# Moving loads, crossbar transposes and state updates between slots of a hand-ordered schedule

## The chip, the core and the metric

The kernel runs on one core of a Trainium2 chip. The metric is the device time of one execution in microseconds. Five executions of the kernel before are at hand, with a median of 217.74 us. Times inside the profile count from the first instruction of one profiled execution.

## What is computed

Causal attention with a decay, in blocks, followed by a two-layer MLP with ELU. The reference, cut to what matters:

```python
batch, n_heads, seq, head_dim = (4, 8, 768, 64)
for b in range(nb):                       # blocks of the sequence
    intra = einsum('bhic,bhjc->bhij', qb, kb) * Dmask
    intra = einsum('bhij,bhjd->bhid', intra, vb)
    inter = einsum('bhid,bhde->bhie', qb * lam_pow, kv_state)
    out[:, :, sl] = intra + inter
    kv_state = lam_block * kv_state + einsum('bhsd,bhse->bhde', kb * rev_pow, vb)
x = out.transpose(0, 2, 1, 3).reshape(3072, 512)
h = x @ w_in                              # 512 x 2048
g = where(h > 0, h, exp(min(h, 0)) - 1)
return g @ w_out                          # 2048 x 512
```

Everything goes in and comes out in float32; the matmuls work in float16.

## The kernel before

The sequence is cut into six chunks of 128 positions. A group g is one chunk of one batch element (g = 4 * chunk + batch), so there are 24 groups. Each turns into 128 rows of the MLP's input. Groups are handled two at a time ("group 10" below is the pair 10 and 11), and the MLP works on seven tiles of TS = 4, 2, 4, 4, 4, 4, 2 groups.

For a pair of groups the attention does the following, one function for each:

- `emit_load` (line 61): three DMAs from GpSimd's queue (POOL) bring q, k and v from HBM, cast to float16 (qn, kn, vn).
- q and k are transposed to qT and kT. For groups up to 6 TensorE does it (`att_T`, `att_Te`), from group 8 on two transposing DMAs from SyncE's queue (SP), the crossbar transposes (`att_xT`, line 272, issued at line 277).
- `att_kd` (line 283) scales k by the decay (kd), on VectorE (DVE) or, for group 8, ScalarE (ACT).
- `att_S` (line 303): scores psS of one group on TensorE (PE, line 308); `att_mask` (line 314) multiplies by the decay mask on DVE, giving P (line 320).
- `att_O` (line 326): output psO of both groups from P and v (line 334) and from qT and the state st (line 342). `att_X` copies it, scaled, to xt, the MLP's input, on DVE (line 363). These are the copies that the change's name speaks of.
- `att_U` (line 369): the state's increment psU from kd and v (line 380). `att_st` (line 404) updates the state st on DVE, in eight instructions (line 418). The next chunk of the same batch elements, four groups on, reads it.

The MLP: `mm1` gives one 128-column slice n of psH for a tile t (line 441; line 459 for the tiles of two groups). ACT takes exp (line 470, e) and relu (line 474, r) of it, and DVE joins them to g (`elu`, line 487). `mm2` (line 519) adds slice n of g times wo to psM for one group of the tile; after the 16th slice psM is copied to osb (DVE at line 533, ACT at line 535; six buffers) and stored from SP's queue (line 536).

The order of the instructions on every engine is the order of the program; nothing reorders them. It is written out by hand in the list `steps`: each entry is a slot, such as (2, 5), with the `mm1` of that slot, then what `at(slot, ...)` has put there, run by `do(s)`, then `elu`, then the slot's list of `mm2`. Within a slot, what was put there first runs first. `visit(g, s0, s1, s2)` puts a pair's parts into three slots: kd in s0, scores and masks in s1, output, increment, copy and update in s2. The table `XT` says in which slot a pair's crossbar transposes are emitted; that fixes their place in SP's queue relative to the stores.

Loads of groups 10 and up are paced: `paced_load` (line 659) has POOL first copy one element of a g made one step earlier (line 665), so that the three DMAs after it start no earlier than that g.

Scores, outputs and increments share the PSUM tag "S", two buffers of two banks; psM and psH have two banks each. With `bufs=3`, qT and kT have three buffers each, which the pairs use in turn.

Of the kernel before, what the change touches and what calls it, by code (L numbers as in the profile page):

```python
# [7 lines left out]
FP32 = mybir.dt.float32  # L8
FP16 = mybir.dt.float16
I32 = mybir.dt.int32  # L10
AF = mybir.ActivationFunctionType
ALU = mybir.AluOpType
# [3 lines left out]
def kernel(  # L16
# [10 lines left out]
    nc = tc.nc  # L27

    B, H, S, D = q.shape
    L = 128  # L30
    HP = H // 2
# [5 lines left out]
    TS = [4, 2, 4, 4, 4, 4, 2]  # L37
# [8 lines left out]
    asb = ctx.enter_context(tc.tile_pool(name="asb", bufs=2))  # L46
    msb = ctx.enter_context(tc.tile_pool(name="msb", bufs=1))
# [67 lines left out]
    def run_loads(items):  # L115
# [25 lines left out]
        out=ident16[:], in0=rel[:], scalar1=0.0, scalar2=None, op0=ALU.is_equal  # L141
    )
    nc.vector.tensor_scalar(
        out=causT[:], in0=rel[:], scalar1=0.0, scalar2=None, op0=ALU.is_ge
# [81 lines left out]
    def att_Te(g, n, which, eng):  # L226
        j = "qk".index(which)
        pt = pT.pop((g, j))
        dst = asb.tile([128, n, HP, 128], FP16, tag=f"{which}T", name=f"{which}T{g}", bufs=3)
        if eng == "v":  # L230
            nc.vector.tensor_copy(dst[:], pt)
        else:
            nc.scalar.copy(out=dst[:], in_=pt)
        for i in range(n):
            (qT, kT)[j][g + i] = dst[:, i]

    def att_T2(g, which, tag):

        j = "qk".index(which)
        nat = heads((qn, kn)[j], g)  # L240
        dst = asb.tile([128, 1, HP, 128], FP16, tag=f"{which}T", name=f"{which}T{g}", bufs=3)
        w = HP // 2
        for x in range(2):
            t1 = ps.tile([128, w, 128], FP16, tag=tag, bufs=2, name=f"psT{which}{g}_{x}")
            for y in range(w):
                hp = x * w + y
                nc.tensor.transpose(
                    t1[:, y, :], in_=nat[:, 2 * hp : 2 * hp + 2, :], identity=ident16[:]
                )
            copy = nc.vector.tensor_copy if x else nc.scalar.copy  # L250
            copy(out=dst[:, 0, x * w : (x + 1) * w], in_=t1[:])
        (qT, kT)[j][g] = dst[:, 0]
# [19 lines left out]
    def att_xT(g):  # L272

        for j, ts in enumerate((qn, kn)):
            w = "qk"[j]
            dst = asb.tile([128, 2 * HP, 128], FP16, tag=f"{w}T", name=f"{w}T{g}", bufs=3)
            nc.sync.dma_start_transpose(
                out=dst[:], in_=heads(ts, g, 2).rearrange("p h d -> p (h d)")
            )
            for i in range(2):  # L280
                (qT, kT)[j][g + i] = dst[:, i * HP : (i + 1) * HP]
# [150 lines left out]
    def mm1_mm(t, n, lo, hi, tag="H"):  # L432

        if n == 0 and lo == 0:
            gt[t] = msb.tile([128, NF, TS[t] * L], FP16, tag="g", bufs=2, name=f"g{t}")
        if lo == 0:
            pH_of[t, n] = ps.tile([128, TS[t] * L], FP32, tag=tag, bufs=2, name=f"psH{t}_{n}")
        pH = pH_of[t, n]
        wi, j = wi_t[wi_at[n][0]], wi_at[n][1]
        for kk in range(HP):  # L440
            nc.tensor.matmul(  # L441
                pH[:, lo:hi], lhsT=wi[:, kk, j * 128 : (j + 1) * 128],
                rhs=xt[t][:, kk, lo:hi], start=(kk == 0), stop=(kk == HP - 1),
            )

    def mm1(t, n, alt=False):

        MT = TS[t] * L
        if MT == 256:
            if n == 0:  # L450
                gt[t] = msb.tile([128, NF, MT], FP16, tag="g", bufs=2, name=f"g{t}")
            pH = ps.tile(
                [128, 2 * MT], FP32, tag="M" if (t, n) in ((1, 0),) else "H", bufs=2,
                name=f"psH{t}_{n}",
            )
            for x in range(2):
                wi, j = wi_t[wi_at[n + x][0]], wi_at[n + x][1]
                for kk in range(HP):
                    nc.tensor.matmul(  # L459
                        pH[:, x * MT : (x + 1) * MT],  # L460
                        lhsT=wi[:, kk, j * 128 : (j + 1) * 128],
                        rhs=xt[t][:, kk, :], start=(kk == 0), stop=(kk == HP - 1),
                    )
            MT *= 2
        else:
            if (t, n) not in pH_of:
                mm1_mm(t, n, 0, MT, "M" if t == 0 and n % 2 == 0 and n < 8 else "H")
            pH = pH_of.pop((t, n))
        e = msb.tile([128, MT], FP32, tag="e", bufs=3, name=f"e{t}_{n}")
        nc.scalar.activation(e[:], pH[:], AF.Exp)  # L470
        if alt:
            return e, None, pH
        r = msb.tile([128, MT], FP16, tag="r", bufs=3, name=f"r{t}_{n}")
        nc.scalar.activation(r[:], pH[:], AF.Relu)  # L474
        return e, r, pH

    def elu(t, n, e, r, pH):
# [11 lines left out]
        )  # L489

    def mm2_last(t, i):

        c, b = divmod(T0[t] + i, B)
        t0 = b * S + c * L
        x0 = 0
        for x, (w, tag) in enumerate([(384, 'M'), (128, 'H')]):
            pm = ps.tile([128, w], FP32, tag=tag, bufs=2, name=f"psM{t}_{i}_{x}")
            for n in range(NF):
                nc.tensor.matmul(  # L499
                    pm[:], lhsT=gt[t][:, n, i * L : (i + 1) * L],  # L500
                    rhs=wo_t[wo_at[n][0]][:, wo_at[n][1], x0 : x0 + w],
                    start=(n == 0), stop=(n == NF - 1),
                )
            o = msb.tile([128, w], FP32, tag="osb", bufs=6, name=f"osl{x}")
            (nc.scalar.copy if x % 2 else nc.vector.tensor_copy)(o[:], pm[:])
            (nc.scalar if x % 2 else nc.sync).dma_start(
                out=out[t0 : t0 + L, x0 : x0 + w], in_=o[:]
            )
            x0 += w
# [47 lines left out]
    def at(s, f, *a, **k):  # L557
        run.setdefault(s, []).append(lambda: f(*a, **k))

    def do(s):  # L560
        for f in run.pop(s, []):
            f()
# [41 lines left out]
    op_Te(3, "k")  # L604
    cut = {}
    for x, f in zip([('O', 0), ('S', 3), ('qs', 0), ('O', 1), ('qs', 1), ('O', 2), ('qs', 2), ('qs', 3), ('O2', 3, 'S'), ('L', 0, 384)], W[8:]):
        warm(f, "M" if not cut else "S")
        if x[0] == "O":
            att_O(x[1], 1, "M" if x[1] < 2 or not cut else "S")
            att_X(x[1], 1)  # L610
        elif x[0] == "S":
            att_S(x[1])
            att_mask(x[1], 2)
        elif x[0] == "qs":
            late_qs(x[1], x[1] + 1)
        elif x[0] == "O2":
            att_OX2(x[1], x[2])
        elif x[0] == "L":
            lo = cut.get(x[1], 0)
            mm1_mm(0, x[1], lo, x[2], "M" if x[1] % 2 == 0 else "H")  # L620
            cut[x[1]] = x[2]

    run_loads(LOADS[16:28])
# [7 lines left out]

    XT = {8: ('B', 12), 10: (1, 12), 12: (2, 4), 14: (2, 12), 16: (3, 4), 18: (3, 12), 20: (4, 4), 22: (4, 12)}
    TMPS = {}

    def visit(g, s0, s1, s2):
        if g in XT:
            at(XT[g], att_xT, g)
        else:
            at(s0, att_T, g, 2, "q")
            at(s0, att_T, g, 2, "k")  # L640
            at(s0, att_Te, g, 2, "q", "a")
            at(s0, att_Te, g, 2, "k", "v" if g in () else "a")
        if g not in ():
            at(s0, att_kd, g, 2, "p" if g in () else "a" if g in (8,) else "v")
        at(s1, att_S, g)
        at(s1, att_S, g + 1)
        at(s1, att_mask, g)
        at(s1, att_mask, g + 1)
        if g in ():
            at(s1, att_kd, g, 2, "p" if g in () else "a" if g in (8,) else "v")  # L650
        at(s2, att_O, g, 2)
        at(s2, att_U, g)
        at(s2, att_X, g, 2)
        at(s2, att_st, g)
        at(TMPS.get(g, s2), att_tmp, g + B)

# [10 lines left out]

    for s, a, b in [(('B', 2), 28, 29), ((1, 2), 29, 30), ((1, 10), 30, 31), ((2, 3), 31, 32), ((2, 11), 32, 33), ((3, 3), 33, 34), ((3, 11), 34, 35), ((4, 3), 35, 36)]:
        at(s, paced_load, s, LOADS[a:b])

    steps = [(('A', 0), (0, 0), []), (('A', 1), (0, 1), []), (('A', 2), (0, 2), []), (('A', 3), (0, 3), []), (('A', 4), (0, 4), []), (('A', 5), (0, 5), []), (('A', 6), (0, 6), []), (('A', 7), (0, 7), []), (('A', 8), (0, 8), []), (('A', 9), (0, 9), []), (('A', 10), (0, 10), [(0, 0, 0), (0, 1, 0)]), (('A', 11), (0, 11), [(0, 0, 1), (0, 1, 1)]), (('A', 12), (0, 12), [(0, 0, 2), (0, 1, 2)]), (('A', 13), (0, 13), [(0, 0, 3), (0, 1, 3)]), (('A', 14), (0, 14), [(0, 0, 4), (0, 1, 4)]), (('A', 15), (0, 15), [(0, 0, 5), (0, 1, 5)]), (('B', 0), None, [(0, 2, 0), (0, 2, 1), (0, 2, 2), (0, 2, 3)]), (('B', 1), None, [(0, 2, 4), (0, 2, 5), (0, 3, 0), (0, 3, 1)]), (('B', 2), None, [(0, 3, 2), (0, 3, 3), (0, 3, 4), (0, 3, 5)]), (('B', 3), None, [(0, 0, 6), (0, 1, 6), (0, 2, 6), (0, 3, 6)]), (('B', 4), None, [(0, 0, 7), (0, 1, 7), (0, 2, 7), (0, 3, 7)]), (('B', 5), None, [(0, 0, 8), (0, 1, 8), (0, 2, 8), (0, 3, 8)]), (('B', 6), None, [(0, 0, 9), (0, 1, 9), (0, 2, 9), (0, 3, 9)]), (('B', 7), None, [(0, 0, 10), (0, 1, 10), (0, 2, 10), (0, 3, 10)]), (('B', 8), None, [(0, 0, 11), (0, 1, 11), (0, 2, 11), (0, 3, 11)]), (('B', 9), None, [(0, 0, 12), (0, 1, 12), (0, 0, 13), (0, 1, 13)]), (('B', 10), None, [(0, 0, 14), (0, 1, 14), (0, 0, 15), (0, 1, 15)]), (('B', 11), None, [(0, 2, 12), (0, 3, 12), (0, 2, 13), (0, 3, 13)]), (('B', 12), None, [(0, 2, 14), (0, 3, 14), (0, 2, 15), (0, 3, 15)]), ((1, 0), (1, 0), []), ((1, 2), (1, 2), []), ((1, 4), (1, 4), []), ((1, 6), (1, 6), [(1, 0, 0), (1, 1, 0), (1, 0, 1), (1, 1, 1)]), ((1, 8), (1, 8), [(1, 0, 2), (1, 1, 2), (1, 0, 3), (1, 1, 3)]), ((1, 10), (1, 10), [(1, 0, 4), (1, 1, 4), (1, 0, 5), (1, 1, 5)]), ((1, 12), (1, 12), [(1, 0, 6), (1, 1, 6), (1, 0, 7), (1, 1, 7)]), ((1, 14), (1, 14), [(1, 0, 8), (1, 1, 8), (1, 0, 9), (1, 1, 9)]), ((2, 0), (2, 0), [(1, 0, 10), (1, 0, 11)]), ((2, 1), (2, 1), [(1, 0, 12), (1, 0, 13)]), ((2, 2), (2, 2), [(1, 0, 14), (1, 0, 15), (1, 1, 10)]), ((2, 3), (2, 3), [(1, 1, 11), (1, 1, 12)]), ((2, 4), (2, 4), [(1, 1, 13), (1, 1, 14)]), ((2, 5), (2, 5), [(1, 1, 15), (2, 0, 0), (2, 0, 1)]), ((2, 6), (2, 6), [(2, 0, 2), (2, 0, 3)]), ((2, 7), (2, 7), [(2, 0, 4)]), ((2, 8), (2, 8), [(2, 0, 5), (2, 1, 0)]), ((2, 9), (2, 9), [(2, 0, 6), (2, 1, 1)]), ((2, 10), (2, 10), [(2, 0, 7), (2, 1, 2)]), ((2, 11), (2, 11), [(2, 0, 8), (2, 1, 3)]), ((2, 12), (2, 12), [(2, 0, 9), (2, 1, 4)]), ((2, 13), (2, 13), [(2, 0, 10), (2, 1, 5)]), ((2, 14), (2, 14), [(2, 0, 11), (2, 1, 6)]), ((2, 15), (2, 15), [(2, 0, 12), (2, 1, 7)]), ((3, 0), (3, 0), [(2, 0, 13), (2, 1, 8), (2, 0, 14), (2, 1, 9)]), ((3, 1), (3, 1), [(2, 0, 15), (2, 1, 10), (2, 1, 11), (2, 1, 12)]), ((3, 2), (3, 2), [(2, 1, 13), (2, 1, 14), (2, 1, 15), (2, 2, 0)]), ((3, 3), (3, 3), [(2, 2, 1), (2, 2, 2), (2, 2, 3), (2, 2, 4), (2, 2, 5)]), ((3, 4), (3, 4), [(2, 2, 6), (2, 2, 7), (2, 2, 8), (2, 2, 9)]), ((3, 5), (3, 5), [(2, 2, 10), (2, 2, 11), (2, 2, 12), (2, 2, 13)]), ((3, 6), (3, 6), [(2, 2, 14), (2, 2, 15), (2, 3, 0), (2, 3, 1), (2, 3, 2)]), ((3, 7), (3, 7), [(2, 3, 3), (2, 3, 4), (2, 3, 5), (2, 3, 6)]), ((3, 8), (3, 8), [(2, 3, 7), (2, 3, 8), (2, 3, 9), (2, 3, 10)]), ((3, 9), (3, 9), [(2, 3, 11), (2, 3, 12), (2, 3, 13), (2, 3, 14), (2, 3, 15)]), ((3, 10), (3, 10), [(3, 0, 0), (3, 0, 1), (3, 0, 2), (3, 0, 3)]), ((3, 11), (3, 11), [(3, 0, 4), (3, 0, 5), (3, 1, 0), (3, 0, 6)]), ((3, 12), (3, 12), [(3, 1, 1), (3, 0, 7), (3, 1, 2), (3, 0, 8), (3, 1, 3)]), ((3, 13), (3, 13), [(3, 0, 9), (3, 1, 4), (3, 0, 10), (3, 1, 5)]), ((3, 14), (3, 14), [(3, 0, 11), (3, 1, 6)]), ((3, 15), (3, 15), [(3, 0, 12), (3, 1, 7)]), ((4, 0), (4, 0), [(3, 0, 13), (3, 1, 8), (3, 0, 14), (3, 1, 9)]), ((4, 1), (4, 1), [(3, 0, 15), (3, 1, 10), (3, 1, 11), (3, 1, 12)]), ((4, 2), (4, 2), [(3, 1, 13), (3, 1, 14), (3, 1, 15), (3, 2, 0)]), ((4, 3), (4, 3), [(3, 2, 1), (3, 2, 2), (3, 2, 3), (3, 2, 4), (3, 2, 5)]), ((4, 4), (4, 4), [(3, 2, 6), (3, 2, 7), (3, 2, 8), (3, 2, 9)]), ((4, 5), (4, 5), [(3, 2, 10), (3, 2, 11), (3, 2, 12), (3, 2, 13)]), ((4, 6), (4, 6), [(3, 2, 14), (3, 2, 15), (3, 3, 0), (3, 3, 1), (3, 3, 2)]), ((4, 7), (4, 7), [(3, 3, 3), (3, 3, 4), (3, 3, 5), (3, 3, 6)]), ((4, 8), (4, 8), [(3, 3, 7), (3, 3, 8), (3, 3, 9), (3, 3, 10)]), ((4, 9), (4, 9), [(3, 3, 11), (3, 3, 12), (3, 3, 13), (3, 3, 14), (3, 3, 15)]), ((4, 10), (4, 10), [(4, 0, 0), (4, 0, 1), (4, 0, 2), (4, 0, 3)]), ((4, 11), (4, 11), [(4, 0, 4), (4, 0, 5), (4, 1, 0), (4, 0, 6)]), ((4, 12), (4, 12), [(4, 1, 1), (4, 0, 7), (4, 1, 2), (4, 0, 8), (4, 1, 3)]), ((4, 13), (4, 13), [(4, 0, 9), (4, 1, 4), (4, 0, 10), (4, 1, 5)]), ((4, 14), (4, 14), [(4, 0, 11), (4, 1, 6)]), ((4, 15), (4, 15), [(4, 0, 12), (4, 1, 7)]), ((5, 0), (5, 0), [(4, 0, 13), (4, 1, 8), (4, 0, 14), (4, 1, 9)]), ((5, 1), (5, 1), [(4, 0, 15), (4, 1, 10), (4, 1, 11), (4, 1, 12)]), ((5, 2), (5, 2), [(4, 1, 13), (4, 1, 14), (4, 1, 15), (4, 2, 0)]), ((5, 3), (5, 3), [(4, 2, 1), (4, 2, 2), (4, 2, 3), (4, 2, 4), (4, 2, 5)]), ((5, 4), (5, 4), [(4, 2, 6), (4, 2, 7), (4, 2, 8), (4, 2, 9)]), ((5, 5), (5, 5), [(4, 2, 10), (4, 2, 11), (4, 2, 12), (4, 2, 13)]), ((5, 6), (5, 6), [(4, 2, 14), (4, 2, 15), (4, 3, 0), (4, 3, 1), (4, 3, 2)]), ((5, 7), (5, 7), [(4, 3, 3), (4, 3, 4), (4, 3, 5), (4, 3, 6)]), ((5, 8), (5, 8), [(4, 3, 7), (4, 3, 8), (4, 3, 9), (4, 3, 10)]), ((5, 9), (5, 9), [(4, 3, 11), (4, 3, 12), (4, 3, 13), (4, 3, 14), (4, 3, 15)]), ((5, 10), (5, 10), [(5, 0, 0), (5, 0, 1), (5, 0, 2), (5, 0, 3)]), ((5, 11), (5, 11), [(5, 0, 4), (5, 0, 5), (5, 1, 0), (5, 0, 6)]), ((5, 12), (5, 12), [(5, 1, 1), (5, 0, 7), (5, 1, 2), (5, 0, 8), (5, 1, 3)]), ((5, 13), (5, 13), [(5, 0, 9), (5, 1, 4), (5, 0, 10), (5, 1, 5)]), ((5, 14), (5, 14), [(5, 0, 11), (5, 1, 6)]), ((5, 15), (5, 15), [(5, 0, 12), (5, 1, 7)]), ((6, 0), (6, 0), [(5, 0, 13), (5, 1, 8), (5, 0, 14), (5, 1, 9), (5, 0, 15)]), ((6, 2), (6, 2), [(5, 1, 10), (5, 1, 11), (5, 1, 12), (5, 1, 13), (5, 1, 14)]), ((6, 4), (6, 4), [(5, 1, 15), (5, 2, 0), (5, 2, 1), (5, 2, 2), (5, 2, 3), (5, 2, 4)]), ((6, 6), (6, 6), [(5, 2, 5), (5, 2, 6), (5, 2, 7), (5, 2, 8), (5, 2, 9)]), ((6, 8), (6, 8), [(5, 2, 10), (5, 2, 11), (5, 2, 12), (5, 2, 13), (5, 2, 14)]), ((6, 10), (6, 10), [(5, 2, 15), (5, 3, 0), (5, 3, 1), (5, 3, 2), (5, 3, 3), (5, 3, 4)]), ((6, 12), (6, 12), [(5, 3, 5), (5, 3, 6), (5, 3, 7), (5, 3, 8), (5, 3, 9)]), ((6, 14), (6, 14), [(5, 3, 10), (5, 3, 11), (5, 3, 12), (5, 3, 13), (5, 3, 14), (5, 3, 15)]), (('E', 0), None, [(6, 0, 0), (6, 0, 1), (6, 0, 2), (6, 0, 3), (6, 0, 4), (6, 0, 5), (6, 0, 6), (6, 0, 7), (6, 0, 8), (6, 0, 9), (6, 0, 10), (6, 0, 11), (6, 0, 12), (6, 0, 13), (6, 0, 14), (6, 0, 15), (6, 1, 0), (6, 1, 1), (6, 1, 2), (6, 1, 3), (6, 1, 4), (6, 1, 5), (6, 1, 6), (6, 1, 7), (6, 1, 8), (6, 1, 9), (6, 1, 10), (6, 1, 11), (6, 1, 12), (6, 1, 13), (6, 1, 14), (6, 1, 15)])]
    for s, m1, m2 in steps:
        er = None
        if m1 is not None:
            t, n = m1
            if t == 0 and n in cut:
                mm1_mm(0, n, cut[n], TS[0] * L)
            er = mm1(t, n, alt=t == 0 and n in (2, 4, 6))
        do(s)
        if er:  # L680
            elu(t, n, *er)
        for t2, i2, n2 in m2:
            mm2(t2, i2, n2, "H" if t2 == 0 and m1 is None and i2 > 1 else "M")
# [31 lines left out]
```

## Time and profile before

| what | us |
|---|---|
| median of five runs | 217.74 |
| the five runs | 213.72, 217.94, 218.27, 213.56, 217.74 |
| the profiled execution | 213.72 |
| its span, first to last instruction | 212.0 |
| busy: PE, DVE, ACT, POOL | 203.0, 148.0, 128.3, 61.9 |
| DMA issue to landing, q of a pair, median | 7.2 |
| DMA issue to landing, transposes of q and of k, median | 4.8, 4.8 |

In the profile's rows, "L441" is line 441 of the kernel. A row of the timeline gives start and length in us, engine, line, operation, what it writes and reads, its form, the number of instructions merged into it, and in brackets how long the engine had been idle before it and what ended that. Matmuls overlap each other in such rows: a 128x512 one is shown with 0.38 us, while the next starts 0.216 us after it. A queue's rows (SPq) are the issuing of DMAs; their landing is given apart. The chain of waits is the work that ended last, followed back to its start.

### The profile page before, as it was taken

Reading aid. Unit: us, or ns where it says so; the run is one execution under the profiler, and the core shown is the slowest. Engines: PE = TensorE matmul, PEld = TensorE weight load, DVE = VectorE, ACT = ScalarE, POOL = GpSimd, SP = SyncE. Lnnn points to the kernel's source line nnn. Section 1 sums busy time; section 2 is a strip of 40 time slices with the busy share of each in tenths; the row PEclk is TensorE's granted clock in tenths of the full one; section 3 lists DMA queues with packets and bytes.
Section 4 is the critical chain, followed back from the end, with each engine's and each line's share of the span. In section 5 each row is a group of like instructions: output and inputs, shape, how many; then the busy total and the mean of one; then the engine's idle time right before and its main releaser. Section 6 shows DMA issues by size and latency. Waiting matters only on the chain.

```text
span 212.0 us, 4157 instructions
## 1 busy us (share of the span) xinstructions
PE 203.0 (96%) x1654; PEld 107.4 (51%) x1654; DVE 148.0 (70%) x240; ACT 128.3 (61%) x247; POOL 61.9 (29%) x70
## 2 busy tenths in 40 slices
PE   4887999999999999999999999999999999999994
PEld 2653444556865453534544544544544544466643
DVE  6674896566989999998698598677557634344321
ACT  6787788406784767666464666464567476675520
POOL 8999965400445070330600700600000000011000
PEclk9999999999999999999999999999999999999999
DMA  5999999999999999895699991799401111011112
GB/s 36 144 152 180 182 199 164 200 157 184 246 134 166 153 129 176 93 122 80 107 154 145 128 116 53 112 152 145 89 0 52 50 49 49 5 49 49 49 53 101
DMA packets 100756, 24.40 MB, mean 115 GB/s; under 512 B 93056, under 2 KB 97920, under 8 KB 100736
## 3 DMA queue, kind: packets, MB, share of 16 engines
q0 software_dynamic: 80384, 14.16, 85.3%
q1 hardware_dynamic: 20208, 9.90, 21.5%
q8 instruction: 13, 0.21, 0.4%
q10 hardware_dynamic: 144, 0.07, 0.1%
q14 instruction: 7, 0.06, 0.1%
HBM read 27.27 MB, written 6.29 MB: 158 GB/s over the span
## 4 chain that ended last, share of the span: by engine, by line
PE 81%; POOL 6%; DVE 5%; DMA 3%; ACT 2%; issue 1%; POOLq 0%; ACTq 0%
PE psM L519 36%; PE psH L441 30%; PE psH L459 5%; DMA wi<-in_moe_w_in_dram 3%; PE psO L334 2%; PE psS L308 2%; PE psO L342 2%; POOL qn L72 2%; POOL kn L72 2%; PE psM L499 2%; POOL vn L72 2%; DVE g L487 1%; DVE xt L363 1%; DVE P L320 1%; ACT kd L293 1%; PE psU L380 1%
## 5 line engine op out<-in xcount | busy, mean ns | idle before, releaser
L519 PE MATMUL psM<-wo,g 128*128 128x512 f16 x368 | 94.2, 380 | 0.3 <-DVE osb L533 0.3
L470 ACT ACTIVATE e<-psH 128x512 f32<-128x512 f32 x96 | 57.3, 597 | 60.2 <-PE psH L441 51.2
L487 DVE SCALAR_TENSOR_TENSOR g<-e,r 128x512 f16<-128x512 f32 x93 | 63.4, 698 | 37.2 <-ACT r L474 36.9
L441 PE MATMUL psH<-xt,wi 128*128 128x512 f16 (+2 forms) x324 | 81.4, 377 | 1.7 <-DMA wi<-in_moe_w_in_dram 1.3
L474 ACT ACTIVATE r<-psH 128x512 f16<-128x512 f32 x93 | 55.1, 593 | 0.0
L519 PEld LDWEIGHTS <-g 128*128 128x128 f16 x368 | 34.2, 98 | 38.7 <-DVE g L487 1.9
L441 PEld LDWEIGHTS <-wi 128*128 128x128 f16 x324 | 31.1, 98 | 40.1 <-DMA wi<-in_moe_w_in_dram 1.8
L320 DVE TENSOR_TENSOR P<-psS,mask 128x1024 f16<-128x1024 f32 (+1 forms) x28 | 28.7, 1066 | 5.8 <-PE psS L308 5.7
L665 POOL COPY pace<-g 1x1 f16<-1x1 f16 x7 | 2.8, 397 | 68.7 <-DVE g L487 68.7
L418 DVE SCALAR_TENSOR_TENSOR st<-st,up_p,psU 64x128 f16<-64x128 f16 x64 | 18.2, 344 | 0.1
L536 POOL DMA_DIRECT2D out_dram<-osb x2 | 1.1, 570 | 56.0 <-ACT osb L535 51.9
L363 DVE TENSOR_TENSOR xt<-psO,qs 128x1024 f16<-128x1024 f32 x10 | 12.2, 1224 | 7.2 <-PE psO L342 7.2
L459 PE MATMUL psH<-xt,wi 128*128 128x256 f16 x128 | 16.4, 273 | 0.0
L72 POOL DMA_DIRECT2D qn<-in_q_dram x14 | 15.3, 1094 | 3.7 <-DMA wi<-in_moe_w_in_dram 1.7
L72 POOL DMA_DIRECT2D vn<-in_v_dram x14 | 15.3, 1108 | 1.8 <-DMA wo<-in_moe_w_out_dram 1.8
L72 POOL DMA_DIRECT2D kn<-in_k_dram x14 | 15.3, 1091 | 1.3 <-DMA kn<-in_k_dram 1.1
L459 PEld LDWEIGHTS <-wi 128*128 128x128 f16 x128 | 12.4, 98 | 4.2
L535 ACT COPY osb<-psM 128x512 f32<-128x512 f32 x12 | 7.1, 591 | 12.2 <-PE psM L519 12.2
L334 PEld LDWEIGHTS <-vn 128*64 128x64 f16 x184 | 9.5, 109 | 4.5 <-issue 4.2
L334 PE MATMUL psO<-P,vn 128*64 128x128 f16 x184 | 11.5, 222 | 0.1
L342 PE MATMUL psO<-qT,st 128*64 128x128 f16 x160 | 10.0, 219 | 0.0
L547 PE MATMUL psW<-ident 128*128 128x256 f16 x34 | 8.0, 360 | 1.7 <-DVE ident L140 1.7
(58 smaller groups left out, 118.8 us busy)
## 6 DMA issues: line engine op xcount, KB each, us to landing
out_dram<-osb SPq DMA_DIRECT2D x21, 256.0 KB, 2.3
qn<-in_q_dram POOLq DMA_DIRECT2D x10, 256.0 KB, 7.2
kn<-in_k_dram POOLq DMA_DIRECT2D x10, 256.0 KB, 9.0
vn<-in_v_dram POOLq DMA_DIRECT2D x10, 256.0 KB, 9.1
wo<-in_moe_w_out_dram POOLq DMA_DIRECT2D x3, 512.0 KB, 14.4
wi<-in_moe_w_in_dram POOLq DMA_DIRECT2D x2, 512.0 KB, 8.3
wi<-in_moe_w_in_dram POOLq DMA_DIRECT2D x3, 256.0 KB, 6.8
qn<-in_q_dram POOLq DMA_DIRECT2D x4, 128.0 KB, 4.8
```

The costliest lines, as they stand in the source:

```text
L72: nc.gpsimd.dma_start(out=dst, in_=src[b : b + n, :, rows].rearrange("b h p d -> p (b h) d"))
L320: nc.vector.tensor_tensor(out=P[:, :, c], in0=s[:, :, c], in1=(mask if g < B else mask1)[:, :, c], op=ALU.mult,)
L334: nc.tensor.matmul(po[r, i, hp, :], lhsT=v_of(g + i, 2 * hp + hh), rhs=P[:, hh, hp, :], start=True, stop=(c == 0), skip_group_check=True,)
L342: nc.tensor.matmul(po[r, i, hp, :], lhsT=st[(g + i) % B // 2][c % 2][:, (g + i) % 2, hp, r], rhs=qT[g + i][:, hp, :], start=False, stop=Tr ...
L363: nc.vector.tensor_tensor(out=dst, in0=po[:, :, c], in1=qs[:, c].unsqueeze(1).broadcast_to([128, n, w, 128]), op=ALU.mult,)
L418: nc.vector.scalar_tensor_tensor(out=new[r, :, hp, r], in0=old[r, :, hp, r], scalar=up_p[r, hp : hp + 1], in1=pu[r, :, hp, :], op0=ALU.mul ...
L441: nc.tensor.matmul(pH[:, lo:hi], lhsT=wi[:, kk, j * 128 : (j + 1) * 128], rhs=xt[t][:, kk, lo:hi], start=(kk == 0), stop=(kk == HP - 1),)
L459: nc.tensor.matmul(pH[:, x * MT : (x + 1) * MT], lhsT=wi[:, kk, j * 128 : (j + 1) * 128], rhs=xt[t][:, kk, :], start=(kk == 0), stop=(kk = ...
L470: nc.scalar.activation(e[:], pH[:], AF.Exp)
L474: nc.scalar.activation(r[:], pH[:], AF.Relu)
L487: nc.vector.scalar_tensor_tensor(out=g, in0=e[:], scalar=-1.0, in1=r[:], op0=ALU.add, op1=ALU.min)
L519: nc.tensor.matmul(pm[:], lhsT=gt[t][:, n, i * L : (i + 1) * L], rhs=wo_t[wo_at[n][0]][:, wo_at[n][1], :], start=(n == 0), stop=(n == NF - 1),
```

## The change

Four edits, of which three move work between slots. The crossbar transposes of groups 10 and 12 are emitted two slots earlier, at (1, 10) and (2, 2). A table `STS` puts the state updates of groups 8 to 18 into the slot after that of the copy to xt. The paced loads of groups 12 to 22 move one or two slots later, and wait for the g of a later slot. qT and kT get four buffers instead of three. The change also brings a function `elu_cols` and two branches for it, which no entry of the kernel's lists uses; they emit nothing.

```diff
@@ att_Te, att_T2, att_xT: the tiles qT and kT
-... tag=f"{which}T", name=f"{which}T{g}", bufs=3)
+... tag=f"{which}T", name=f"{which}T{g}", bufs=4)
@@
-    XT = {8: ('B', 12), 10: (1, 12), 12: (2, 4), 14: (2, 12), 16: (3, 4), 18: (3, 12), 20: (4, 4), 22: (4, 12)}
+    XT = {8: ('B', 12), 10: (1, 10), 12: (2, 2), 14: (2, 12), 16: (3, 4), 18: (3, 12), 20: (4, 4), 22: (4, 12)}
     TMPS = {}
+    STS = {8: (2, 0), 10: (2, 6), 12: (2, 14), 14: (3, 6), 16: (3, 14), 18: (4, 6)}
@@ visit
         at(s2, att_O, g, 2)
         at(s2, att_U, g)
         at(s2, att_X, g, 2)
-        at(s2, att_st, g)
+        at(STS.get(g, s2), att_st, g)
@@ slot, first and last load of the list
-    for s, a, b in [(('B', 2), 28, 29), ((1, 2), 29, 30), ((1, 10), 30, 31), ((2, 3), 31, 32), ((2, 11), 32, 33), ((3, 3), 33, 34), ((3, 11), 34, 35), ((4, 3), 35, 36)]:
+    for s, a, b in [(('B', 2), 28, 29), ((1, 2), 29, 30), ((1, 14), 30, 31), ((2, 4), 31, 32), ((2, 12), 32, 33), ((3, 4), 33, 34), ((3, 12), 34, 35), ((4, 4), 35, 36)]:
         at(s, paced_load, s, LOADS[a:b])
```

List entry 28 is the load of group 8, 29 that of group 10, 30 that of group 12, and so on to 35, group 22. Of the copies to xt, those of groups 8, 10, 12, 14, 16 and 18 stand in slots (1, 14), (2, 5), (2, 13), (3, 5), (3, 13) and (4, 5).

More of the change, by code (lines that the diff above doesn't have):

```diff
@@ L228, in att_Te @@
         pt = pT.pop((g, j))
-        dst = asb.tile([128, n, HP, 128], FP16, tag=f"{which}T", name=f"{which}T{g}", bufs=3)
+        dst = asb.tile([128, n, HP, 128], FP16, tag=f"{which}T", name=f"{which}T{g}", bufs=4)
         if eng == "v":
@@ L240, in att_T2 @@
         nat = heads((qn, kn)[j], g)
-        dst = asb.tile([128, 1, HP, 128], FP16, tag=f"{which}T", name=f"{which}T{g}", bufs=3)
+        dst = asb.tile([128, 1, HP, 128], FP16, tag=f"{which}T", name=f"{which}T{g}", bufs=4)
         w = HP // 2
@@ L275, in att_xT @@
             w = "qk"[j]
-            dst = asb.tile([128, 2 * HP, 128], FP16, tag=f"{w}T", name=f"{w}T{g}", bufs=3)
+            dst = asb.tile([128, 2 * HP, 128], FP16, tag=f"{w}T", name=f"{w}T{g}", bufs=4)
             nc.sync.dma_start_transpose(
@@ L489, in elu, with elu_cols @@
         )
+    def elu_cols(t, n, lo, hi, alt):
+        pH = pH_of[t, n]
+        w = hi - lo
+        g = gt[t][:, n, lo:hi]
+        e = msb.tile([128, w], FP32, tag="e", bufs=3, name=f"e{t}_{n}_{lo}")
+        nc.scalar.activation(e[:], pH[:, lo:hi], AF.Exp)
+        m = msb.tile([128, w], FP16, tag="r", bufs=3, name=f"m{t}_{n}_{lo}")
+        if alt:
+            nc.vector.tensor_scalar(
+                out=m[:], in0=e[:], scalar1=-1.0, scalar2=0.0, op0=ALU.add, op1=ALU.min
+            )
+            nc.vector.tensor_tensor(out=g, in0=m[:], in1=pH[:, lo:hi], op=ALU.max)
+        else:
+            nc.scalar.activation(m[:], pH[:, lo:hi], AF.Relu)
+            nc.vector.scalar_tensor_tensor(
+                out=g, in0=e[:], scalar=-1.0, in1=m[:], op0=ALU.add, op1=ALU.min
+            )
     def mm2_last(t, i):
@@ L604 @@
     op_Te(3, "k")
-    cut = {}
+    cut, ecut = {}, {}
     for x, f in zip([('O', 0), ('S', 3), ('qs', 0), ('O', 1), ('qs', 1), ('O', 2), ('qs', 2), ('qs', 3), ('O2', 3, 'S'), ('L', 0, 384)], W[8:]):
@@ L621 @@
             cut[x[1]] = x[2]
+        elif x[0] == "E":
+            elu_cols(0, x[1], 0, cut[x[1]], x[2])
+            ecut[x[1]] = cut[x[1]]
     run_loads(LOADS[16:28])
@@ L677 @@
                 mm1_mm(0, n, cut[n], TS[0] * L)
+            if t == 0 and n in ecut:
+                do(s)
+                elu_cols(0, n, ecut[n], TS[0] * L, True)
+                pH_of.pop((0, n))
+                for t2, i2, n2 in m2:
+                    raise AssertionError
+                continue
             er = mm1(t, n, alt=t == 0 and n in (2, 4, 6))
```

## The prediction

> **What bounds the kernel now.** I read the page's busy shares and slices first, then the sums over stretches, then the timelines of PE, DVE, SP and POOL where PE waits.
>
> ```profile
> span 212.0 us, 4157 instructions
> PE 203.0 (96%) x1654; PEld 107.4 (51%) x1654; DVE 148.0 (70%) x240; ACT 128.3 (61%) x247; POOL 61.9 (29%) x70
> ```
>
> The profiled execution took 213.72 us, so 1.7 us lie around its span. It is 4.0 us under the median of the five times (217.74) and close to the lowest (213.56). The five lie in two groups, two at 213.6 to 213.7 and three at 217.7 to 218.3. What the longer ones spent 4 us on is not in this trace, so every sum below stands on 213.72 first.
>
> ```profile
> 56.00:70.00 14.00, 13.90 (x150) 8.73 (x145) 13.38 (x28) 9.27 (x23) 7.47 (x8) 1.00 1.76 169
> 70.00:82.00 12.00, 11.66 (x109) 5.63 (x108) 11.84 (x21) 8.75 (x17) 3.94 (x4) 1.00 1.44 137
> ...
> 97.00:115.00 18.00, 18.00 (x152) 8.78 (x151) 14.33 (x24) 10.51 (x21) 3.62 (x4) 1.00 1.06 118
> 115.00:160.00 45.00, 45.00 (x346) 21.94 (x345) 32.17 (x51) 26.01 (x49) 7.67 (x8) 1.00 0.90 100
> ```
>
> Columns are the stretch, its length, then busy time of PE, PEld, DVE, ACT and POOL, the granted clock, DMA share and GB/s. From 97 us on PE is busy all the time and DVE is not: nothing in the change can win there. Between 56 and 97 us DVE is full too (13.38 of 14, 11.84 of 12). All that this execution can give lies there. PE's timeline shows how much:
>
> ```profile
> 70.67 0.62 PE L308 MATMUL psS<-qT,kT 64*128 64x128 f16 x16
> ...
> 79.73 1.03 PE L441 MATMUL psH<-xt,wi 128*128 128x512 f16 x4
> 80.76 0.39 PE L519 MATMUL psM<-wo,g 128*128 128x512 f16 x1
> 81.48 0.38 PE L519 MATMUL psM<-wo,g 128*128 128x512 f16 x1 [0.33 <-DVE osb L533]
> ...
> 93.82 1.21 PE L519 MATMUL psM<-wo,g 128*128 128x512 f16 x4
> ```
>
> A full 128x512 matmul follows the last after 0.216 us (four in 0.86 in the chain). So the row at 79.73 is issued by 80.59 and the next waits 0.17 (for g of slot (2,5), ready at 80.70); the one at 81.48 comes 0.50 late (for the psM bank that osb frees at 81.42); at 93.82 there are 0.17, and 0.16 inside that row. With 0.27 at 67.11 (xt of tile 2) that is 1.27 us, the ceiling for this execution.
>
> ```profile
> 76.55 1.23 DVE L363 TENSOR_TENSOR xt<-psO,qs 128x1024 f16<-128x1024 f32 x1
> 77.69 2.28 DVE L418 SCALAR_TENSOR_TENSOR st<-st,up_p,psU 64x128 f16<-64x128 f16 x8
> 80.01 0.69 DVE L487 SCALAR_TENSOR_TENSOR g<-e,r 128x512 f16<-128x512 f32 x1
> 80.73 0.69 DVE L533 COPY osb<-psM 128x512 f32<-128x512 f32 x1
> ...
> 89.61 1.23 DVE L363 TENSOR_TENSOR xt<-psO,qs 128x1024 f16<-128x1024 f32 x1 [0.51 <-PE psO L342]
> ```
>
> The state update, 2.28 us that nothing needs soon, stands ahead of the g and the osb that PE waits for.
>
> **The change part by part.** *State updates one slot later* (groups 8 to 18; the same eight instructions). At (2,5) g and osb now follow xt at once: ready at 78.4 and 79.1 instead of 80.70 and 81.42. PE's 0.17 and 0.50 go: 0.67 us. The update runs 79.1 to 81.4, and g of (2,6), behind it, keeps its 81.34. Not all 0.67 stays, for DVE has no idle time until 89.11: there it waits 0.51 for PE's psO. PE 0.67 earlier lets xt of group 12 start at 89.11, 0.50 earlier. The sequence to g of (2,14), which PE waits for, is equally long in either order, so that g comes at 93.86 instead of 94.36, and PE passes there 0.50 earlier. Net gain 0.5 us. Bounds: 0 (DVE gives nothing back) to 1.0 (also the 0.33 at 93.8). What is late next: psU is held longer. At (2,0) the update of group 8 ends at 69.95 instead of 69.25, and its bank is wanted by the second score of group 10 at 70.97: 1.0 us to spare, cost 0. In tiles 3 to 5 PE has no wait left to remove.
>
> *Transposes of 10/11 at (1,10), of 12/13 at (2,2).* In SP's list the pair of group 10 keeps its neighbours, after tile 0's last stores. SP already stands there:
>
> ```profile
> SPq L277 <- DMA qn<-in_q_dram: 6.3, 2, 5.9
> ```
>
> ```profile
> 61.83 1.25 SPq L277 DMA_TRANSPOSE qT<-qn  x1
> 63.69 1.43 SPq L277 DMA_TRANSPOSE kT<-kn  x1
> 72.48 0.33 SPq L536 DMA_DIRECT2D out_dram<-osb  x1
> 72.91 1.30 SPq L277 DMA_TRANSPOSE qT<-qn  x1
> ```
>
> ```profile
> DMA to landing us min/median/max: 6.7/6.7/6.7
> ```
>
> These are SP's waits, SP's timeline, and the time to landing of group 10's kT (issued at 63.7). SP waits 5.9 us for qn, which lands at 61.8, and kT follows kn at 63.7. Moving this pair changes nothing. The pair of group 12 passes one store (72.48), which now waits behind it; six osb buffers stand behind the store, so 0.
>
> *Loads later.* The load of group 12 hangs on g of (1,12) (65.88) instead of (1,8) (62.29): its issues move from 62.99 to about 66.6. In the trace they share the DMA engines with group 10's transposes: kT takes 6.66 us and lands at 70.36, 0.3 us ahead of the scores at 70.67. Alone, kT takes 3.1 (groups 12, 22). With the load 3.6 later I take 4.5 (qT of 10 took 4.6): landing 68.2, margin 2.4 us; gain in this execution 0. The load itself, by the row of group 10's (5.3, 6.1, 6.6 us to landing), lands at 71.9, 73.9 and 75.5; qT and kT of 12 issue at 71.9 and 73.9, and even at group 14's 5.4 us kT is there at 79.3, 4.0 ahead of the scores (83.9, less 0.67). The other loads move by one g, 0.6 to 1.2 us; those of 18 and 22 still meet transposes of 16 and 20 (kT 9.7 and 9.4 us, 1.0 and 1.2 us ahead of need), a little later. Cost 0, margins somewhat wider.
>
> A rule of the Trainium skill speaks against this part (SBUF — State Buffer, "SBUF: two separate sides"): while VectorE runs a two-port op, GpSimd is locked out and cannot write descriptors. The load's issues move beside the update and kd of group 10 (1.22). The row: the 14 qn issues took 896 to 1212 ns, those at 88.6 beside DVE's xt and update 1.15. By the rule each of the three could wait for an op of 1.22, 3.7 us in all, and kT of 12 would land at about 83, just at the need; by the row it is 0. I take the row, and keep the other for a rival.
>
> *Four qT/kT buffers.* With three, qT of 12 reuses that of group 6, last read at 55.9; no wait to remove: 0.
>
> Sum: 213.72 - 0.5 = **213.2 us**, for an execution like the profiled one.
>
> **Rivals.** *My forecast: the median comes down to 213.2.* The only transfer with next to no margin is kT of group 10, and the change takes the load away from it. In the trace a kT beside a load takes up to 9.7; here that would be 3.0 us more (73.4 instead of 70.4), near the 4 us between the groups of times; small shifts between load and transposes can decide which of them is served first. With the load moved, the long executions lose this. For it: the 0.3 us. Against: it is not seen in this trace. Chance 0.57; own range 212.4 to 213.8.
>
> *The 4 us sit elsewhere and stay.* Before 56 us both programs have the same order, and PE waits for loads there (1.3 us for wi at 20.3; kT of 8 follows kn that took 14.9 us to land). If the long executions lose their time there, the median stays: 217.74 - 0.5 = 217.2. This is also the case in which the change does not do what it says. Chance 0.30.
>
> *Slower: group 12 is late instead.* If its load lands as slowly as kn at 134.5 (9.4 us), kn is there at 77.1, kT issues at 77.2, and with 9.7 lands at 86.9 against scores wanted at 83.9: 3.0 us stall, 217.74 + 3.0 = 220.7. It decides when kT of 12 takes over 6.7. The skill says (DMA: Bandwidth & Descriptors, "SWDGE vs HWDGE vs iDMA") that an engine takes turns between software and hardware queues: two streams would double 3.1 to 6.2, landing at 83.4, no stall. The rows say 9.4 to 9.7, so the stall is possible, but needs slow load and slow transpose at once, with no other load due before 76. Chance 0.05.
>
> The remaining 0.08 lie between, at 213.8 to 216.5.
>
> **How the numbers follow.** Likeliest 213.2. The range takes in the first two cases: 212.4 (gain of 1.0 and a little) to 218.3 (the highest time, gain 0). Two per cent, about what a measurement of this kernel tells from no change, lie at 213.4 and 222.1. My forecast's case falls under 213.4 in four of five: faster 0.46. The rest of it, the second case, the space between and most of the third are within: 0.51. Slower 0.03.
>
> **What would show it.** Right: g of (2,5) before st in DVE's order with no PE gap near 80; PE at the row of 93.82 about 0.5 us sooner; kT of 10 landing near 68; SP still waiting about 6 us for qn; PE full from 97 on. Wrong: scores of 10 or 12 waiting for kT; DVE idle before a g of (1,14), (2,5) or (2,13); PE gaps before 56 us that differ, or a median still near 217.

## The result and the profile after

The changed kernel takes 212.83 us (median of 28 runs, 212.31 to 213.14). The kernel before, now with 49 runs, takes 215.2 us (213.07 to 220.98). The ratio of the two is 0.9943, with a 95% interval of 0.993 to 0.9956; it leaves out executions more than 1.5% above the fastest of their kernel, and these are what the change removed, so it does not show the whole effect: the medians of all runs stand at 212.83 / 215.2 = 0.989. Of the 49 runs before, 26 took 213.07 to 215.2 us and 23 took 217.3 to 220.98, with none between; the highest of the 28 after is 213.14.

The profiled execution took 212.78 us. Its page opens with:

```profile
span 211.0 us, 4157 instructions
PE 202.5 (96%) x1654; PEld 106.8 (51%) x1654; DVE 148.4 (70%) x240; ACT 128.5 (61%) x247; POOL 61.5 (29%) x70
```

The stretches (length, then busy PE, PEld, DVE, ACT, POOL, granted clock, DMA share, GB/s):

```profile
70.00:82.00 12.00, 12.00 (x111) 5.93 (x110) 11.88 (x21) 8.66 (x17) 3.94 (x4) 1.00 1.59 152
82.00:97.00 15.00, 14.82 (x137) 7.24 (x135) 14.35 (x24) 10.25 (x20) 3.94 (x4) 1.00 1.62 129
```

PE has no idle time left from 70 to 82 (11.66 became 12.00), and 0.18 in the next stretch. (Before, that stretch read 14.99 of 15.00; its waits of 0.33 us near 93.8 could be told only from the distance of the rows.) PE's and DVE's timelines show where that comes from:

```profile
79.12 0.38 PE L538 MATMUL psM<-wo,g 128*128 128x512 f16 x1
79.34 1.03 PE L441 MATMUL psH<-xt,wi 128*128 128x512 f16 x4
80.20 0.59 PE L538 MATMUL psM<-wo,g 128*128 128x512 f16 x2
...
82.97 0.62 PE L308 MATMUL psS<-qT,kT 64*128 64x128 f16 x16
...
93.45 0.61 PE L538 MATMUL psM<-wo,g 128*128 128x512 f16 x2 [0.18 <-DVE g L487]
```

```profile
76.16 1.23 DVE L363 TENSOR_TENSOR xt<-psO,qs 128x1024 f16<-128x1024 f32 x1
77.30 0.68 DVE L487 SCALAR_TENSOR_TENSOR g<-e,r 128x512 f16<-128x512 f32 x1
77.90 0.69 DVE L552 COPY osb<-psM 128x512 f32<-128x512 f32 x1
78.50 2.29 DVE L418 SCALAR_TENSOR_TENSOR st<-st,up_p,psU 64x128 f16<-64x128 f16 x8
```

The next g and osb come ahead of the 2.29 us of st, and the two matmuls that had waited 0.17 and 0.50 us are now one row at 80.20. (Line 538 is the old 519, 552 the old 533.) At 93.45 a wait remains: the row before it is issued by 93.11, so 0.34 us.

How much of the difference between the two profiled executions is the change's? The scores of group 12 come at 83.94 before and 82.97 after, 0.97 us sooner. At 40 us, ahead of all that the change moves, PE was already 0.39 sooner (40.88 and 40.49). From the scores of group 10 to those of group 12 it is 13.27 us before and 12.69 after (82.97 less 70.28): the change wins 0.58 us, and the rest is another course of the first 40 us.

SP's waits and timeline, and the time to landing of group 10's kT:

```profile
SPq L277 <- DMA qn<-in_q_dram: 14.8, 4, 5.6
```

```profile
62.29 1.25 SPq L277 DMA_TRANSPOSE qT<-qn  x1
64.16 1.25 SPq L277 DMA_TRANSPOSE kT<-kn  x1
70.97 1.24 SPq L277 DMA_TRANSPOSE qT<-qn  x1
```

```profile
DMA to landing us min/median/max: 4.8/4.8/4.8
```

SP still waits 5.6 us for qn of group 10, so emitting its pair earlier did nothing. It now waits as long for qn of group 12 too, and the stores behind are issued from 74.90 on instead of 72.48. The kT of 10 takes 4.8 us instead of 6.7 and lands at 68.9, 1.4 us ahead of its scores (70.28). The pair of group 12 is issued at 70.97 and 73.42; kT lands 3.5 us later, 6.0 ahead of its scores at 82.97.

### The profile page after: what moved, and what is told of

Its sections match the earlier page's. It is cut to its first block, busy times and chain, and to the rows that moved or that the text cites. A ratio compares the mean times of both kernels' runs of the same rounds, so it can differ in the third digit from the quotient of the medians.

```text
span 211.0 us, 4157 instructions
## 1 busy us (share of the span) xinstructions
PE 202.5 (96%) x1654; PEld 106.8 (51%) x1654; DVE 148.4 (70%) x240; ACT 128.5 (61%) x247; POOL 61.5 (29%) x70
## 4 chain that ended last, share of the span: by engine, by line
PE 75%; POOL 11%; DMA 6%; DVE 3%; ACT 2%; issue 1%; POOLq 0%; ACTq 0%
PE psM L538 34%; PE psH L441 26%; DMA kn<-in_k_dram 6%; PE psH L459 5%; POOL wi L97 2%; PE psO L334 2%; PE psS L308 2%; POOL qn L72 2%; PE psO L342 2%; POOL kd L295 2%; POOL kn L72 2%; PE psM L518 2%; POOL vn L72 2%; DVE g L487 1%; DVE P L320 1%; ACT kd L293 1%
## 5 line engine op out<-in xcount | busy, mean ns | idle before, releaser
L487 DVE SCALAR_TENSOR_TENSOR g<-e,r 128x512 f16<-128x512 f32 x93 | 64.2, 704 | 37.3 <-ACT r L474 37.0
L688 POOL COPY pace<-g 1x1 f16<-1x1 f16 x7 | 2.3, 329 | 68.9 <-DVE g L487 68.9
```

The source lines that it names most:

```text
L487: nc.vector.scalar_tensor_tensor(out=g, in0=e[:], scalar=-1.0, in1=r[:], op0=ALU.add, op1=ALU.min)
```

## The experiments

All start from the kernel before unless said otherwise. Theory A, the prediction's: the load of group 12, beside the transposes of group 10, makes the long executions; the place of the state update makes the 0.5 us. Its rivals, the theories B to E, are told in the expectations. The runs of the kernel before on the same chips spread each time, 213.1 to 221.5.

**The parts alone.** Later loads:

```diff
- ((1, 10), 30, 31), ((2, 3), 31, 32), ((2, 11), 32, 33), ((3, 3), 33, 34), ((3, 11), 34, 35), ((4, 3), 35, 36)
+ ((1, 14), 30, 31), ((2, 4), 31, 32), ((2, 12), 32, 33), ((3, 4), 33, 34), ((3, 12), 34, 35), ((4, 4), 35, 36)
```

> The kernel before with the later loads alone. Theory A (the load of group 12 beside the transposes of group 10 makes the long executions, the state update's place makes the 0.5 us): the times lose their upper part, none above about 214.5, median 213.2 to 213.7, and the two PE gaps near 80 us stay. Theory B (the place of the state update makes the long executions): times still spread to 218, median 214 to 218. Theory C (the earlier transposes of group 12 do it): as B.

Measured: 213.57 us (12 runs, 212.69 to 213.94). The spread is gone, as A has it; B and C fall as sole causes. The PE gaps near 80 us stay (0.18 and 0.50 by the distance of the rows):

```profile
80.65 0.39 PE L519 MATMUL psM<-wo,g 128*128 128x512 f16 x1
81.37 0.38 PE L519 MATMUL psM<-wo,g 128*128 128x512 f16 x1 [0.33 <-DVE osb L533]
```

Later state updates:

```diff
-        at(s2, att_st, g)
+        at({8: (2, 0), 10: (2, 6), 12: (2, 14), 14: (3, 6), 16: (3, 14), 18: (4, 6)}.get(g, s2), att_st, g)
```

> The kernel before with the later state updates alone. Theory A: the PE gaps near 80 us go, the lowest times come down by 0.5 us to about 213.0, but the times still spread up to about 218. Theory B: no time above about 213.5. Theory C: as A.

Measured: 214.33 us (212.33 to 222.48). The lowest time is that of the changed kernel (212.31), and the spread stays. In its trace PE's gaps near 80 us are gone: from the scores of group 10 to those of group 12 it is 12.70 us (73.65 to 86.35), as in the changed kernel, against 13.28 with the later loads alone.

Earlier transposes:

```diff
- 10: (1, 12), 12: (2, 4)
+ 10: (1, 10), 12: (2, 2)
```

> The kernel before with the transposes of groups 10 and 12 two slots earlier alone. Theory A: nothing changes, lowest about 213.5, spread up to 218. Theory B: the same. Theory C: no time above about 214.5.

Measured: 215.38 us (213.27 to 220.36), as the kernel before in median and spread. C falls.

**The change without its loads** (the other three edits):

> The changed kernel with the loads back where they were before. Theory A: spread up to 217 or 218 again, lowest about 212.6. Theories B and C: no spread, median about 212.9.

Measured: 213.94 us (212.72 to 220.65). The spread is back.

**A long execution seen.** The profiled execution of the kernel with the earlier transposes alone took 219.11 us. Up to the scores of group 10 its order is that of the kernel before. PE's timeline:

```profile
69.30 1.03 PE L441 MATMUL psH<-xt,wi 128*128 128x512 f16 x4
74.46 1.00 PE L308 MATMUL psS<-qT,kT 64*128 64x128 f16 x16 [4.13 <-DMA kT<-kn]
75.39 1.46 PE L519 MATMUL psM<-wo,g 128*128 128x512 f16 x3
76.64 1.68 PE L441 MATMUL psH<-xt,wi 128*128 128x512 f16 x4
78.16 0.59 PE L519 MATMUL psM<-wo,g 128*128 128x512 f16 x2
78.59 1.03 PE L441 MATMUL psH<-xt,wi 128*128 128x512 f16 x4
```

PE stands 4.13 us until kT of group 10 lands. After it, the scores take 1.00 us, three matmuls 1.46 and four 1.68, and the next row starts 3.70 us after the scores. In the kernel before it is 2.07:

```profile
70.67 0.62 PE L308 MATMUL psS<-qT,kT 64*128 64x128 f16 x16
71.22 0.82 PE L519 MATMUL psM<-wo,g 128*128 128x512 f16 x3
71.88 1.03 PE L441 MATMUL psH<-xt,wi 128*128 128x512 f16 x4
72.74 0.60 PE L519 MATMUL psM<-wo,g 128*128 128x512 f16 x2
```

The stretch from 75 to 78 says why (the clock is the number before the last two):

```profile
75.00:78.00 3.00, 3.00 (x17) 1.15 (x12) 2.93 (x3) 0.59 (x1) 0.00 (x0) 0.51 0.95 185
```

The granted clock is 0.51. So one late transpose costs 4.1 us of wait and then 1.6 us at half clock. POOL's issue of the k of group 12, SP's of kT of group 10, and the landing of that kT:

```profile
63.71 1.16 POOL L72 DMA_DIRECT2D kn<-in_k_dram  x1
```

```profile
64.78 1.60 SPq L277 DMA_TRANSPOSE kT<-kn  x1
```

```profile
DMA to landing us min/median/max: 9.6/9.6/9.6
```

Here kT follows the k of group 12 by 1.07 us, because kn of group 10 landed at 64.77; in the first profile it landed at 63.67, and kT was issued 0.43 ahead. Which comes first is open in each execution: kT's issue hangs on a landing, the load's on g. (That landing of kn moves between 63.2 and 65.5 us over the fourteen profiles; why, stays open.) The profiles of all runs, some of them of experiments told below, nearly line up by that distance:

| kernel | issue of kT of 10 after that of k of 12, us | kT to landing, us | PE's wait for kT, us |
|---|---|---|---|
| earlier transposes alone | +1.07 | 9.63 | 4.1 |
| load 12 earlier, at (1,8) | +1.06 | 9.33 | 2.6 |
| later state updates alone | 0.00 | 8.88 | 2.3 |
| the other loads later | +0.02 | 7.76 | 1.2 |
| change without its loads | -0.44 | 6.95 | none, 0.04 to spare |
| before | -0.43 | 6.66 | none |
| load 12 at (1,12) | -1.65 | 4.75 | none |
| two edits for four | -1.76 | 4.95 | 0.2 |
| changed kernel | -3.17 | 4.76 | none |
| all loads later, without and with the state updates | -3.50, -3.55 | 3.23, 3.37 | none |
| load 12 later, alone | -3.87 | 3.32 | none |
| changed kernel, one update further | -4.16 | 3.29 | none |
| load 12 at (2,2) | -10.32 | 3.24 | none |

**Which load.** That of group 12 alone (`(1, 10), 30, 31` to `(1, 14), 30, 31`):

> The kernel before with the load of group 12 alone moved, from (1,10) to (1,14). Theory A (this one load, beside kT of group 10, makes the long executions): no time above about 214.5, median 213.5, as with all loads moved. Theory D (the loads of 14 to 22 matter too, beside the transposes of 16 and 20): times up to 216 or more remain.

Measured: 213.46 us (12 runs, 213.17 to 214.70). None over 215; two at 214.5 and 214.7 are a little above what A expected. The one at 214.7 has a mean granted clock of 0.992, as the long execution above; there is no trace of it, and what slowed its clock is not shown.

The other five alone (`(2, 3)` to `(2, 4)` and so on, `(1, 10)` left):

> The kernel before with the loads of groups 14 to 22 moved one slot later, that of 12 left. Theory A: as the kernel before, lowest about 213.5, spread up to 218 or more. Theory D: the spread shrinks by half or more.

Measured: 214.59 us (213.33 to 220.51). D falls: it is the one load.

**The collision forced.** `(1, 10), 30, 31` to `(1, 8), 30, 31`:

> The kernel before with the load of group 12 one slot earlier, at (1,8), where its k is issued about 1 us ahead of kT of group 10 instead of about 0.4 us after it. Theory A: kT now queues behind that load in every execution: it lands 9 to 10 us after its issue, scores of group 10 wait 2.5 to 4.5 us, median 217 to 219 and no time under about 215. Theory E (the long executions are rare bad luck of the DMA engines, not a matter of order): the same spread as before, lowest 213.5.

Measured: 217.99 us (6 runs, 215.94 to 222.32): no execution escapes. PE's waits from 60 to 120 us:

```profile
PE psS L308 <- DMA kT<-kn: 2.6, 1, 2.6
PE psM L519 <- DVE osb L533: 0.3, 1, 0.3
```

E falls: the order of issue decides. One slot later instead, `(1, 12), 30, 31`:

> The kernel before with the load of group 12 one slot later, at (1,12), where its q is issued near 65 us, about 1 us after kT of group 10. Theory A: the order is now settled in nearly every execution; highest time under 215.5, median 213.5 to 214. If a load one slot away still disturbs, times up to 218 remain.

Measured: 213.52 us (12 runs, 212.98 to 215.78). Nearly all settled; the highest is 0.3 over what was expected, again at a clock of 0.992 and without a trace.

**The load too late.** `(1, 10), 30, 31` to `(2, 2), 30, 31`:

> The kernel before with the load of group 12 five slots later, at (2,2): issued near 72.5 us. Group 10 is quite free. Now the transposes of group 12 have to wait for kn at about 79, and the next load falls on them. If a load can come too late here, scores of group 12 (wanted at 83.9) wait and the median rises above 214.5, with all times up; if not, the times are those of the load at (1,14), 213.5.

Measured: 221.81 us (6 runs, 220.73 to 223.18), slower than any other kernel here. In its profile the scores of group 12 wait, and their kT takes 9.8 us. The three views are PE's wait, the stretches from 86 to 92 us, and the time to landing:

```profile
89.57 1.03 PE L308 MATMUL psS<-qT,kT 64*128 64x128 f16 x16 [6.19 <-DMA kT<-kn]
```

```profile
86.00:89.00 3.00, 0.00 (x0) 0.00 (x0) 0.00 (x0) 0.00 (x0) 0.00 (x0) 0.50 1.68 167
89.00:92.00 3.00, 2.43 (x20) 1.36 (x21) 1.78 (x2) 0.00 (x0) 0.00 (x0) 0.50 1.40 183
```

```profile
DMA to landing us min/median/max: 9.8/9.8/9.8
```

Here the half clock is granted during the wait already. That is the prediction's slower rival: kT of 12 was issued at 79.78, behind the loads of both 12 and 14. So the load has a window: at (1,10) it meets the transposes of 10, at (2,2) the load of 14 meets those of 12.

**Two edits for four**: load of group 12 at (1,14), later state updates, nothing else.

> The kernel before with two edits alone: the load of group 12 at (1,14) and the later state updates; transposes, other loads and three buffers as before. Theory A: all of the change's effect, median 212.8, none above 213.3. Theory D, or one in which the earlier transposes or the fourth buffer count: slower than the changed kernel by 0.3 us or more, or with times above 214.

Measured: 213.05 us (12 runs, 212.68 to 213.46), 0.2 above the changed kernel. In its profile kn of group 10 landed at 65.47, later than in the long execution (64.77), yet kT landed at 70.43 and PE waited 0.22 us for it. So a late kn alone does not make a long execution; the load beside it does.

All loads later and later state updates, transposes and three buffers as before:

> All loads later and the state updates later; transposes as before, three buffers. If the earlier transposes of group 12 and the fourth buffer do nothing: median 212.8, as the changed kernel. If they give the 0.2 us between the changed kernel and the two edits alone: 213.0 to 213.1.

Measured: 213.03 us (12 runs, 212.39 to 213.75). Between this and 212.83 lies the most that the earlier transposes of group 12 and the fourth buffer can be worth. The ranges overlap, and the two were not run side by side; whether it is 0.2 or nothing stays open.

**Further.** The changed kernel with the state update of group 12 a slot further:

```diff
-    STS = {8: (2, 0), 10: (2, 6), 12: (2, 14), ...
+    STS = {8: (2, 0), 10: (2, 6), 12: (3, 0), ...
```

> The changed kernel with the state update of group 12 one slot further, at (3,0): g of (2,14) no longer stands behind it. If PE's wait of 0.34 us near 93.5 is set by that order: 0.3 us off, median 212.5. If DVE is simply full there, the wait moves to the next g and the median stays at 212.8.

Measured: 212.51 us (6 runs, 212.40 to 212.98), the lowest median of all, though its range overlaps with the changed kernel's. PE's and DVE's timelines:

```profile
91.87 1.03 PE L441 MATMUL psH<-xt,wi 128*128 128x512 f16 x4
92.74 1.03 PE L519 MATMUL psM<-wo,g 128*128 128x512 f16 x4
```

```profile
92.76 0.69 DVE L487 SCALAR_TENSOR_TENSOR g<-e,r 128x512 f16<-128x512 f32 x1 [0.60 <-ACT r L474]
93.37 2.29 DVE L418 SCALAR_TENSOR_TENSOR st<-st,up_p,psU 64x128 f16<-64x128 f16 x8
```

The four matmuls at 92.74 run without the 0.34 us. The g ahead of them no longer stands behind st, and DVE waits for ACT: it was not full there, its order was wrong.

## Why the prediction was right, and where not

The time, 212.83 against 213.2, and its cause were right. That the cause was the load of group 12 was a guess at 0.57 when it was made; the experiments above show it.

*State updates, 0.5 us.* Right in place and size. With the loads moved, the later updates took the median from 213.57 to 213.03, and with load 12 alone from 213.46 to 213.05: 0.5 and 0.4. The traces have 0.57 and 0.58 from the scores of group 10 to those of group 12. The step "the sequence to g of (2,14) is equally long in either order" held: PE waits 0.34 for it now and 0.33 before. The 0.17 us that the prediction let DVE take back there it did not take. That this was DVE being full was read too quickly; only st stood in between, as the last run shows.

*Transposes of group 10: nothing.* Right: SP waits for qn as before, and the edit alone gave 215.38 against 215.37. Those of group 12: no cost, as said; a gain of up to 0.2 is open.

*Load of group 12.* Its issue was put at 66.6 and came at 66.19; landings of 5.3, 6.1 and 6.6 us were taken and were 4.7, 6.1 and 6.5. kT of 10 was put at 68.2 and came at 68.9; that of 12 at 79.3, and came at 76.9. The lock rule for the descriptors was weighed and not taken, and nothing of it is seen: the three issues beside DVE's st and kd took 1.15, 1.16 and 1.18 us, as before. Whether st or kd is a two-port op, no run here shows.

*"The long executions lose this."* The likeliest case is what happened: the kT with 0.3 us to spare, and the order of issue that decides. Its size was put at 3.0 us (2.7 of wait, with 0.3 to spare), and the 4 us to the upper group were left half explained. The traces show 1.2 to 4.1 us of wait, by the distance in the table, and on top 1.6 us at half clock after the longest. That term is missing from the prediction's sum. The Trainium skill (TensorE: Matmul & The Clock Gate, "HAM oscillation — how this bites in real kernels") names idle gaps over about 3.4 us as what brings the half rate. Here the waits of 4.1 and 6.2 us did (granted clock 0.51 and 0.50), those of 2.3 and 2.6 us did not (1.00). The clocks of whole executions leave a doubt: of 87 runs of the kernel before that list them, the 61 from 213.1 to 217.3 us have 0.998 or more, and the 26 from 216.4 on have 0.992 or less. An execution of 216.4 us has lost only 3.3 us in all, half clock included, so a shorter wait may be enough, or its half clock came elsewhere; none like it was traced.

*The base.* The two groups read from five times hold in the 49 runs, with nothing between 215.2 and 217.3, and the half clock fits as what sets the upper one apart, though the clocks of these 49 are not listed. On other chips the space between is filled in part (215.6, 216.4, 216.8). But the five held three of the upper group, while of the 49 it has 23, so the median is 215.2 and stands at the top of the lower group. So the step from 217.74 to 213.2 was too large a fall, though both ends are right for single executions: in medians the gain is 1.1%, within 2%, and my 0.46 for more leaned on a median of five.

*Rivals.* That the 4 us sit before 56 us is refuted: none of the 28 runs after is long, and the profiles with a late kT lose their time between 69 and 78 us. The slower one is real as a mechanism, with 9.8 us for kT, where two streams in turn were put at 6.2; in the changed kernel kT of 12 lands 6 us ahead of its scores. Its sum of 220.7 put the stall of 3.0 us on top of 217.74; with the long executions gone, as the change makes them, the same stall on 213.2 would have given 216.2, within 2% of the base.

*The other loads* were said to widen margins somewhat. kT of 16 and 20 now take 7.2 and 7.3 us instead of 9.7 and 9.4, now that their qT is issued ahead of the load (about 7.0 to 7.3 in every trace with those loads later, 9.1 to 9.9 in every other), and land 3.4 us before their scores; it gives no time that the runs could show (214.59 with these loads alone later, 215.06 before).

## What to carry to other kernels

A transfer that lands 0.3 us before its use is no hidden transfer: look for what is issued in the same microsecond on another queue, and give its issue a distance that the jitter of a landing cannot bridge. When times of one kernel spread by per cents, profile a long one, and shift the suspected transfer both ways: the way that makes all executions long names the cause. On an engine that others wait for, put work that nobody wants soon behind what they wait for, even where the sum of its work stays the same.

## What was not expected

A transpose's time hangs on the order of issue to within a microsecond: 3.2 to 3.4 us when it is issued 3.5 us or more ahead of the k of the next load, 4.8 to 5.0 at 1.7 us ahead (and still 4.8 at 3.2), 6.7 to 7.0 at 0.4 us ahead, 7.8 to 8.9 when issued with it, 9.3 to 9.6 when issued 1.1 us behind. And a wait of 4.1 us on PE costs 1.6 us more than itself, at a granted clock of 0.51.
